# Attention with a top-32 mask and an MLP on one core: tile-major order with early MLP chunks, and two heads side by side on TensorE

## The chip, the cores and the metric

The kernel runs on one core of a Trainium2 chip. The metric is the time of one execution on the device, in microseconds (us). Three runs of the kernel before took 2404.17 to 2404.62 us, median 2404.35 us.

## The reference, cut to what matters

```python
# q, k, v: (8 batches, 8 heads, 576 tokens, 64), float32
scores = scale * np.matmul(q, k.transpose(0, 1, 3, 2))          # scale = 1/8
kth = np.partition(scores, -32, axis=-1)[..., -32:-32 + 1]      # the 32nd largest of each row
scores = np.where(scores >= kth, scores, -1000000000.0)
scores = scores - np.max(scores, axis=-1, keepdims=True)
attn = np.exp(scores)
attn = attn / (np.sum(attn, axis=-1, keepdims=True) + 1e-09)
x = np.matmul(attn, v)                                          # heads side by side: x is (4608, 512)
h = x @ w_in                                                    # w_in (512, 2048) and w_out (2048, 512), float64
g = np.where(h >= 1, h, np.where(h <= -1, 0.0, (h + 1) ** 2 / 4))
out = (g @ w_out).astype(np.float32)
```

## The kernel before

All products are float32. The eight batches are worked on as four pairs. Within a pair the loops run over four pairs of heads (`hp`), then nine tiles of 128 queries (`t`), then the two heads of the pair (`j`), so a step is one head of one tile, and there are 288 steps. Tile 4 holds the last 64 queries of the one batch and of the other. The parts of a step are spread over four turns of the main loop (from L285), so that several steps overlap:

- `scores` (L150): TensorE multiplies queries by keys in two halves of 288 keys with 64 rows of contraction, those of head `j` on partitions 64j to 64j + 63. ScalarE copies each half out of PSUM (L161). The PSUM tiles share four buffers, tag `mm`, with the first product of the MLP.
- `top_k` (L164): VectorE takes eight maxima (L171) and strikes them out (L175), four times over, for the 32 largest.
- `weights` (L179): ScalarE takes the exponential (L181); VectorE sets what lies under the 32nd value to zero and sums (L183), and takes the reciprocal of the sum (L187).
- `transpose_w` and `values` (L190, L200): TensorE transposes the weights in six pieces (L196), ScalarE copies them to `wT`, and TensorE multiplies them by the values with `wT` as the stationary operand (L205). ScalarE scales by the reciprocal (L210). After the second head of a pair `transpose_x` turns the 128 columns of `x` (L215).

The weights of the MLP arrive as 64-bit words. `weight_piece` (L68) makes float32 of 512 columns with six VectorE and five GpSimd instructions; there are 32 pieces. They are the side work of the first pair of batches. The MLP of a pair of batches (`mlp`, L219) works in three chunks of three tiles: 16 times four products into `ph` (L226), the activation on ScalarE, GpSimd and VectorE (L230 to L234), then 16 products per tile into `py` (L241). It is the side work of the next pair of batches' attention, and the last pair's MLP follows when all attention is done. `advance` (L271) deals out the side work by a rate.

The order in which each engine sees its instructions is set when the program is built: a scheduler puts instructions of the listing in order by its own estimate of times and by when buffers come free, and the engines then run their queues in that order.

Of the kernel before, what the change touches and what calls it, by code (L numbers as in the profile page):

```python
# [19 lines left out]
def kernel(  # L20
# [9 lines left out]
    """moe_w_in and moe_w_out are float64 arrays, seen as 64-bit integers; all else is float32."""  # L30
# [5 lines left out]
    assert D == 64 and S == 576 and DM == H * D == 512 and NTOK == B * S  # L36
    assert B % 2 == 0 and DFF % 512 == 0 and TOP_K % 8 == 0

    NP = B // 2              # pairs of batches: 1152 tokens, 9 tiles of 128
    NHP = H // 2             # pairs of heads: 128 columns of x  # L40
    NT = 2 * S // P          # query tiles of a pair of batches
    KC, KP = 6, 96           # keys of a head: chunk c, partition p is key KC * p + c
# [5 lines left out]
    NCH = NT // CT  # L48
    SCALE = float(D) ** -0.5

    const = ctx.enter_context(tc.tile_pool(name="const", bufs=1))
# [14 lines left out]
    WC = 512  # L66

    def weight_piece(pool, dst, src):  # L68
# [4 lines left out]
        # sign and top exponent bit, the low 7 exponent bits with 20 mantissa bits, 3 more  # L73
# [6 lines left out]
        # what the 29 bits left are worth: rest * 2^-52 * 2^exponent  # L80
# [4 lines left out]
        # 0 below float32's normal range, whose exponents these bits cannot say  # L85
# [23 lines left out]
    def load(bp, hp):  # L109
        b, h = 2 * bp, 2 * hp  # L110
        q_in = stage.tile([P, NT, 2, D], F32, name="q_in")
        k_in = stage.tile([KP, 2, KC, 2, D], F32, name="k_in")
        v_in = stage.tile([KP, 2, 2, KC, D], F32, name="v_in", bufs=2)
        for j in range(2):
# [5 lines left out]
            for i in range(2):  # L120
                nc.sync.dma_start(out=k_in[:, i, :, j, :], in_=k[b + i, h + j].rearrange("(p c) d -> p c d", p=KP))
# [163 lines left out]
    for m in range(n + 3):  # L285
# [20 lines left out]
        if m < n:  # L306
            top_k(state[m])
# [48 lines left out]
```

## Time and profile before

| | |
|---|---|
| median of three runs | 2404.35 us |
| profiled execution, first to last instruction | 2408.7 us |
| TensorE products (PE) busy | 2325.6 us, 97% |
| TensorE weight loads (PEld) busy | 1438.2 us, 60% |
| VectorE (DVE) busy | 1928.1 us, 80% |
| ScalarE (ACT) busy | 1005.0 us, 42% |
| GpSimd (POOL) busy | 430.8 us, 18% |
| chain of waits, by engine | PE 81%, DVE 12%, POOL 5% |

The span of 2408.7 us is the profiled execution's own time from its first instruction to its last, and it is 4.3 us above the median of the runs. Busy shares are averages over stretches with different limits. A busy PE is one with a product in flight, at whichever clock; the granted clock stands beside it in the slices and the stretches. A float32 product leaves two records, one per pass; a transpose leaves one.

### The profile page before, as it was taken

How to read it: one execution, taken by the hardware profiler on the slowest of the kernel's cores; microseconds unless marked ns; L12 is line 12 of the kernel's file. 1: busy time of each engine (PE TensorE's matmuls, PEld its weight loads, DVE VectorE, ACT ScalarE, POOL GpSimd, SP SyncE). 2: the span in 40 equal slices, each digit the busy share in tenths (PEclk: the TensorE clock that was granted, in tenths of full speed). 3: DMA queues.
4: the chain of work that ended last, by engine and by line, in shares of the span. 5: the costliest groups of instructions: out<-in, count | busy, mean ns of one | idle time of the engine just before them, and what ended most of it. 6: DMA issues, size and time to landing. Idle time of an engine off the chain costs nothing.

```text
span 2408.7 us, 29579 instructions
## 1 busy us (share of the span) xinstructions
PE 2325.6 (97%) x10016; PEld 1438.2 (60%) x10016; DVE 1928.1 (80%) x4416; ACT 1005.0 (42%) x2405; POOL 430.8 (18%) x647
## 2 busy tenths in 40 slices
PE   7888888999999999999999999999999999999999
PEld 4555555667665665655666656656666656565554
DVE  7889989988898898988898898889898988871100
ACT  3333333333544544544544544545545445432211
POOL 3554554200110100100100101101101102001210
PEclk6555555555999999999999999999999999999999
DMA  4111111000001000000000010000010000000000
GB/s 104 48 58 47 54 56 43 20 11 10 20 15 29 11 25 19 18 18 19 11 25 19 11 29 15 21 19 25 11 29 15 11 9 5 5 9 9 5 14 13
DMA packets 93399, 56.44 MB, mean 23 GB/s; under 512 B 78400, under 2 KB 84544, under 8 KB 93248
## 3 DMA queue, kind: packets, MB, share of 16 engines
q1 hardware_dynamic: 93248, 54.54, 8.0%
q8 instruction: 80, 1.31, 0.2%
q14 instruction: 71, 0.58, 0.1%
HBM read 45.09 MB, written 9.44 MB: 23 GB/s over the span
## 4 chain that ended last, share of the span: by engine, by line
PE 81%; DVE 12%; POOL 5%; issue 1%; ACT 0%; SPq 0%; DMA 0%; POOLq 0%; ACTq 0%; DVEq 0%
PE ph L226 21%; PE py L241 21%; PE po L205 15%; PE sp L158 14%; PE pw L196 8%; DVE tops L171 4%; DVE rest L175 3%; POOL low L93 2%; POOL low L92 2%; DVE w L183 2%; POOL keep L89 1%; PE px L215 1%; DVE top L76 1%; DVE top L78 1%; POOL low L91 1%
## 5 line engine op out<-in xcount | busy, mean ns | idle before, releaser
L171 DVE MAX8 tops<-rest 128x8 f32<-128x576 f32 x864 | 650.5, 753 | 8.0
L205 PEld LDWEIGHTS po<-v_in,wT 96*128 96x128 f32 (+1 forms) x3840 | 498.0, 212 | 134.4 <-ACT wT L197 116.9
L226 PE MATMUL ph<-xT,w_in 128*128 128x384 f32 x1536 | 551.9, 497 | 0.0
L241 PE MATMUL py<-w_out,g 128*128 128x512 f32 x1152 | 547.9, 604 | 2.1 <-ACT y L246 2.1
L205 PE MATMUL po<-v_in,wT 96*128 96x64 f32 (+1 forms) x3840 | 522.0, 299 | 2.9 <-ACT wT L197 2.8
L158 PE MATMUL sp<-kT,qT 64*128 64x288 f32 (+1 forms) x1280 | 500.3, 520 | 0.6 <-ACT g L232 0.4
L175 DVE MATCH_REPLACE8 rest<-tops,rest 128x576 f32<-128x576 f32 x576 | 427.7, 743 | 0.0
L226 PEld LDWEIGHTS ph<-xT,w_in 128*128 128x128 f32 x1536 | 274.6, 192 | 169.8 <-issue 31.4
L197 ACT COPY wT<-pw 96x384 f32<-96x384 f32 x576 | 252.8, 477 | 276.4 <-PE pw L196 274.7
L196 PEld LDWEIGHTS pw<-ident,w 128*96 128x96 f32 x1728 | 220.8, 143 | 218.1 <-issue 200.0
L196 PE MATMUL pw<-ident,w 128*96 128x128 f32 x1728 | 287.0, 311 | 64.0 <-DVE w L183 63.3
L234 DVE SCALAR_TENSOR_TENSOR g<-g,r 128x384 f32<-128x384 f32 x192 | 106.8, 556 | 279.3 <-POOL r L233 272.9
L241 PEld LDWEIGHTS py<-w_out,g 128*128 128x128 f32 x1152 | 200.0, 190 | 207.0 <-issue 197.7
L158 PEld LDWEIGHTS sp<-kT,qT 64*128 64x128 f32 (+1 forms) x1280 | 204.5, 204 | 167.4 <-issue 107.1
L171 DVE MAX8 tops<-s 128x8 f32<-128x576 f32 x288 | 215.0, 747 | 100.8 <-ACT s L161 100.6
L233 POOL TENSOR_TENSOR r<-r 128x384 f32<-128x384 f32 x192 | 163.8, 853 | 710.0 <-ACT r L230 706.0
L161 ACT COPY s<-sp 128x288 f32<-128x288 f32 x576 | 207.0, 407 | 190.4 <-DVE w L183 151.3
L173 POOL TENSOR_SCALAR nmax<-tops 128x1 f32<-128x1 f32 x288 | 61.7, 215 | 1084.8 <-DVE tops L171 1084.0
L181 ACT ACTIVATE w<-s,nmax 128x576 f32<-128x576 f32 x288 | 222.3, 772 | 80.2 <-POOL nmax L173 79.5
L210 ACT ACTIVATE x<-po,rz 128x64 f32<-128x64 f32 x288 | 90.1, 313 | 389.4 <-PE po L205 380.7
L183 DVE SCALAR_TENSOR_TENSOR w<-s,tops,w 128x576 f32<-128x576 f32 x288 | 245.3, 852 | 0.1
L175 DVE MATCH_REPLACE8 rest<-tops,s 128x576 f32<-128x576 f32 x288 | 213.7, 742 | 0.0
(37 smaller groups left out, 981.3 us busy)
## 6 DMA issues: line engine op xcount, KB each, us to landing
k_in<-in_k_dram SPq DMA_DIRECT2D x64, 144.0 KB, 3.0
v_in<-in_v_dram SPq DMA_DIRECT2D x32, 288.0 KB, 3.4
out_dram<-y SPq DMA_DIRECT2D x36, 256.0 KB, 2.3
q_in<-in_q_dram SPq DMA_DIRECT2D x64, 128.0 KB, 2.6
raw<-in_moe_w_in_dram SPq DMA_DIRECT2D x16, 512.0 KB, 3.7
raw<-in_moe_w_out_dram SPq DMA_DIRECT2D x16, 512.0 KB, 3.6
q_in<-in_q_dram SPq DMA_DIRECT2D x64, 16.0 KB, 2.1
```

Source lines behind the costliest of these rows:

```text
L158: nc.tensor.matmul(sp[r0:r1], qT[d0:d1, t, r0:r1], kT[d0:d1, i, 3 * hf:3 * hf + 3, :].rearrange("p c n -> p (c n)"), start=True, stop=True)
L161: nc.scalar.copy(s[:, hf * SH:(hf + 1) * SH], sp)
L171: nc.vector.max(out=tops[:, r:r + 8], in_=src)
L175: nc.vector.match_replace(out=rest, in_to_replace=tops[:, r:r + 8], in_values=src, imm_value=LOWEST)
L181: nc.scalar.activation(w, st["s"], AF.Exp, bias=st["nmax"], scale=SCALE)
L183: nc.vector.scalar_tensor_tensor(out=w, in0=st["s"], scalar=st["tops"][:, TOP_K - 1:TOP_K], in1=w, op0=ALU.is_ge, op1=ALU.mult, accum_out=z)
L196: nc.tensor.transpose(pt[:, c, :], w[:, (c0 + c) * KP:(c0 + c + 1) * KP], ident)
L197: nc.scalar.copy(wT[:, c0:c0 + 3, :], pt)
L205: nc.tensor.matmul(po[r0:r1], st["wT"][:, c, r0:r1], heads["v"][:, i, j, c, :], start=(c == 0), stop=(c == KC - 1))
L226: nc.tensor.matmul(ph, w_in[:, kk, f * P:(f + 1) * P], xT[:, kk, ch * CW:(ch + 1) * CW], start=(kk == 0), stop=(kk == NK - 1))
L233: nc.gpsimd.tensor_tensor(out=r, in0=r, in1=r, op=ALU.mult)
L241: nc.tensor.matmul(py, gs[f][:, i * P:(i + 1) * P], w_out[:, f, :], start=(f == 0), stop=(f == NF - 1))
```

## The change

A step is now two heads of one tile, and there are 144 steps. The order is tile-major: for one batch, each tile of 128 queries goes through its four pairs of heads before the next tile begins, so a tile's 512 columns of `x` are complete after four steps. The last 64 queries of two batches share a tile of `x`. An MLP chunk of up to three tiles starts when its tiles are done: the first after 12 steps, with the 32 weight pieces dealt out over those 12 steps. The remaining chunks follow one another as side work, the last with a single tile.

The two heads' scores are issued one after the other, on partitions 0 to 63 and 64 to 127, into two PSUM buffers of a tag of their own (`sc`). The mask is no longer a VectorE instruction: ScalarE applies a leaky rectifier to threshold minus score, with slope 2^-80 on the negative side, and then an exponential with scale -2^80, which gives zero for what lies under the threshold, and sums as it goes. The reciprocal of the sum goes into a diagonal matrix made by GpSimd, and the weights are transposed by an ordinary product with that matrix. In the product with the values the values are stationary, 64 columns per head, and the two heads write to partitions 0 to 63 and 64 to 127 of one PSUM tile; the result has the layout that the MLP wants, and `transpose_x` is gone. In the MLP the copy of `ph` by ScalarE is gone: VectorE reads `ph` from PSUM, and `ph` has two PSUM buffers of its own. The program holds one load of ScalarE's function table, as before.

```diff
-    xtp = ctx.enter_context(tc.tile_pool(name="xtp", bufs=2))
-    stage = ctx.enter_context(tc.tile_pool(name="stage", bufs=1))
-    qkt = ctx.enter_context(tc.tile_pool(name="qkt", bufs=2))
-    att = ctx.enter_context(tc.tile_pool(name="att", bufs=3))
+    xtp = ctx.enter_context(tc.tile_pool(name="xtp", bufs=3))
+    stage = ctx.enter_context(tc.tile_pool(name="stage", bufs=2))
+    att = ctx.enter_context(tc.tile_pool(name="att", bufs=2))
...
+    def keys_of(b):
+        kT = stage.tile([P, NHP, S], F32, name="kT")
...
+            for j in range(2):
+                nc.sync.dma_start(out=k_in[:, :, j, :], in_=whole(k, b)[:, 2 * hp + j])
+            pt = ps.tile([P, NT, P], F32, name="pk", tag="tr", bufs=2)
+            for c in range(NT):
+                nc.tensor.transpose(pt[:, c, :], k_in[:, c].rearrange("p j d -> p (j d)"), ident)
+            nc.scalar.copy(kT[:, hp, 0:SM], pt.rearrange("p c n -> p (c n)"))
...
+            yield dict(kT=kT, v=v_in, v_tl=v_tl)
...
+    def scores(st):
+        t, hp, kT, qT = st["t"], st["hp"], st["keys"]["kT"], st["qT"]
+        st["s"] = s = att.tile([P, 2, S], F32, name="s", bufs=4)
+        for hf in range(2):
+            keys = slice(hf * SH, (hf + 1) * SH)
+            sp = [ps.tile([P, SH], F32, name="sp", tag="sc", bufs=2) for _ in range(2)]
             for i in range(2):
+                for j in ([i] if t < NT else [0, 1]):
+                    d = slice(j * D, (j + 1) * D)
+                    g = hp if t < NT else hp + i
+                    o = sp[i] if t < NT else sp[i][j * TL:(j + 1) * TL]
+                    nc.tensor.matmul(o, qT[d, g, :], kT[d, g, keys], start=True, stop=True)
+            for i in range(2):
+                nc.scalar.activation(s[:, i, keys], sp[i], AF.Copy, scale=SCALE)
...
     def weights(st):
-        w = att.tile([P, S], F32, name="w")
-        nc.scalar.activation(w, st["s"], AF.Exp, bias=st["nmax"], scale=SCALE)
-        z = att.tile([P, 1], F32, name="z")
-        nc.vector.scalar_tensor_tensor(out=w, in0=st["s"], scalar=st["tops"][:, TOP_K - 1:TOP_K], in1=w,
-                                       op0=ALU.is_ge, op1=ALU.mult, accum_out=z)
-        rz = att.tile([P, 1], F32, name="rz")
+        s, tops = st["s"], st["tops"]
+        nb = att.tile([P, 2], F32, name="nb")
+        nc.gpsimd.tensor_tensor(out=nb, in0=tops[:, :, TOP_K - 1], in1=tops[:, :, 0], op=ALU.subtract)
+        z = att.tile([P, 2], F32, name="z")
+        for i in range(2):
+            nc.scalar.activation(s[:, i, :], s[:, i, :], AF.Prelu, bias=tops[:, i, TOP_K - 1:TOP_K], scale=-1.0,
+                                 alpha=1.0 / FAR)
+            nc.scalar.activation(s[:, i, :], s[:, i, :], AF.Exp, bias=nb[:, i:i + 1], scale=-FAR,
+                                 accum_out=z[:, i:i + 1])
+        rz = att.tile([P, 2], F32, name="rz")
         nc.vector.tensor_scalar(z, z, 1e-9, None, ALU.add)
         nc.vector.reciprocal(rz, z)
-        st["w"], st["rz"] = w, rz
+        st["diag"] = diag = att.tile([P, 2, P], F32, name="diag")
+        for i in range(2):
+            nc.gpsimd.tensor_scalar(diag[:, i, :], ident, rz[:, i:i + 1], 1.0, ALU.mult, ALU.mult)
...
     def transpose_w(st):
...
+        t, w, diag = st["t"], st["s"], st["diag"]
+        st["wT"] = wT = att.tile([P, 2, NT, P], F32, name="wT")
+        st["wTt"] = wTt = att.tile([P, P], F32, name="wTt")
+        for i in range(2):
+            pt = ps.tile([P, NT, P], F32, name="pw", tag="tr", bufs=2)
+            for c in range(NT):
+                nc.tensor.matmul(pt[:, c, :], w[:, i, c * P:(c + 1) * P], diag[:, i, :], start=True, stop=True)
+            nc.scalar.copy(wT[:, i], pt)
+        pt = ps.tile([P, P], F32, name="pwt", tag="po")
+        for i in range(2):
+            if t < NT:
+                nc.tensor.matmul(pt[i * TL:(i + 1) * TL], w[:, i, SM:S], diag[:, i, :], start=True, stop=True)
...
+        nc.scalar.copy(wTt, pt)
...
     def values(st):
-        t, j, heads = st["t"], st["j"], st["heads"]
-        po = ps.tile([P, D], F32, name="po", tag="po")
-        for r0, r1, i in rows_of(t):
-            for c in range(KC):
-                nc.tensor.matmul(po[r0:r1], st["wT"][:, c, r0:r1], heads["v"][:, i, j, c, :],
-                                 start=(c == 0), stop=(c == KC - 1))
-        if j == 0:
-            heads["x"] = att.tile([P, P], F32, name="x", bufs=2)
-        st["x"] = x = heads["x"]
-        nc.scalar.activation(x[:, j * D:(j + 1) * D], po, AF.Copy, scale=st["rz"])
...
+        t, hp, v_in, v_tl = st["t"], st["hp"], st["keys"]["v"], st["keys"]["v_tl"]
+        wT, wTt = st["wT"], st["wTt"]
+        po = ps.tile([P, P], F32, name="po", tag="po")
+        if t < NT:
+            for c in range(NT + 1):
+                for j in range(2):
+                    h = 2 * hp + j
+                    nc.tensor.matmul(po[j * D:(j + 1) * D], v_in[:, h, c, :] if c < NT else v_tl[:, h, :],
+                                     wT[:, j, c, :] if c < NT else wTt, start=(c == 0), stop=(c == NT))
...
+    def mlp(xT, tiles, pool):
+        cw = len(tiles) * P
+        gs = []
+        for f in range(NF):
+            ph = ps.tile([P, CW], F32, name="ph", tag="ph", bufs=2)[:, 0:cw]
+            for kk in range(NK):
+                nc.tensor.matmul(ph, w_in[:, kk, f * P:(f + 1) * P], xT[:, kk, 0:cw],
+                                 start=(kk == 0), stop=(kk == NK - 1))
+            r = pool.tile([P, CW], F32, name="r", bufs=2)[:, 0:cw]
+            nc.scalar.activation(r, ph, AF.Relu, bias=half, scale=0.5)
+            g = pool.tile([P, CW], F32, name="g", bufs=NF)
+            nc.gpsimd.tensor_tensor(out=r, in0=r, in1=r, op=ALU.mult)
+            nc.vector.scalar_tensor_tensor(out=g[:, 0:cw], in0=ph, scalar=1.0, in1=r, op0=ALU.max, op1=ALU.min)
+            gs.append(g)
+            yield
...
+    rounds, chunks = [], []
+    for b in range(0, B, 2):
+        a, c, tl = [(b, t) for t in range(NT)], [(b + 1, t) for t in range(NT)], (b, NT)
+        if b + 2 < B:
+            rounds += a + [tl] + c + [(b + 1, NT)]
+            chunks += [a[0:3], a[3:4] + c[0:2], c[2:4] + [tl]]
+        else:
+            rounds += a + [tl, (b + 1, NT)] + c
+            chunks += [a[0:3], a[3:4] + [tl] + c[0:1], c[1:3], c[3:4]]
...
+    begin(0)
+    next_keys = 1
+    for m in range(n + 2):
         if m < n:
             top_k(state[m])
+        if m + 1 < n:
+            begin(m + 1)
         if 1 <= m <= n:
             weights(state[m - 1])
-        if 2 <= m <= n + 1:
+        if 2 <= m:
             transpose_w(state[m - 2])
         advance(rate / 2)
-        if 2 <= m <= n + 1:
...
+        if 2 <= m:
             values(state[m - 2])
-        advance(rate / 2)
-        if 3 <= m:
-            transpose_x(state[m - 3])
-            if (m - 2) % per_bp == 0:
-                done = (m - 2) // per_bp
+            state[m - 2] = None
+            for ch in [c for c in range(len(chunks)) if ready[c] == m - 2]:
                 for _ in side:
                     pass
                 if mlp_pool is None:
                     cvt.__exit__(None, None, None)
                     mlp_pool = ctx.enter_context(tc.tile_pool(name="mlp", bufs=1))
-                side, due, rate = mlp(done - 1, xTs[done - 1], mlp_pool), 0.0, n_units / (per_bp - 2)
-            state[m - 3] = None
+                side, due = mlp(xTs[ch], chunks[ch], mlp_pool), 0.0
+                rate = units[ch] / (ready[ch + 1] - ready[ch]) if ch + 1 < len(chunks) else 0.0```

Two places show how the instructions move. The first is TensorE in the middle of the program. Before, the weights of one head (`pw`), the two halves of scores (`sp`) and one head's values (`po`) alternate with MLP products (`ph`), and only the first `pw` and the first `po` of a group wait:

```order
L196 MATMUL pw<-ident,w 96x128 [waits DVE_49,PE_49]
L196 MATMUL pw<-ident,w 96x128 x2
L196 MATMUL pw<-ident,w 96x128 [waits Activation_49]
L196 MATMUL pw<-ident,w 96x128 x2
L158 MATMUL sp<-kT,qT 128x288
L205 MATMUL po<-v_in,wT 128x64 [waits Activation_49]
L205 MATMUL po<-v_in,wT 128x64 x2
L205 MATMUL po<-v_in,wT 128x64 [waits Activation_49]
L205 MATMUL po<-v_in,wT 128x64 x2
L158 MATMUL sp<-kT,qT 128x288 x3
L226 MATMUL ph<-xT,w_in 128x384 [waits Activation_49]
L226 MATMUL ph<-xT,w_in 128x384 x2
```

Now a whole step of two heads stands in twelve rows (`pwt` is the last 64 keys of the weights):

```order
L181 MATMUL sp<-kT,qT 128x288 x2
L181 MATMUL sp<-kT,qT 128x288 [waits Activation_49] x2
L226 MATMUL pw<-diag,s 128x128 [waits Pool_49]
L226 MATMUL pw<-diag,s 128x128 x3
L226 MATMUL pw<-diag,s 128x128 [waits Pool_49]
L226 MATMUL pw<-diag,s 128x128 x3
L231 MATMUL pwt<-diag,s 64x128 [waits PE_49]
L231 MATMUL pwt<-diag,s 64x128
L277 MATMUL ph<-xT,w_in 128x384 x4
L247 MATMUL po<-wT,v_in 64x128 [waits Activation_49]
L247 MATMUL po<-wT,v_in 64x128 x7
L247 MATMUL po<-wTt,v_tail_79 64x128 x2
```

The second pair of score products now waits for ScalarE to empty the two buffers of the first pair. Of the 132 steps from the first MLP product on, 55 have the second pair directly behind the first, as here, and most of the others have one to four `pw` products in between.

The second place is GpSimd while the weights are converted. Before, one piece (L91 to L94) lies between the small products for the maxima (`nmax`) of one or two steps:

```order
L91 TENSOR_SCALAR low<-rest 128x512
L92 TENSOR_TENSOR low<-low,unit 128x512
L89 TENSOR_SCALAR keep<-keep 128x512
L93 TENSOR_TENSOR low<-low,top 128x512
L94 TENSOR_TENSOR w_in<-low,keep 128x512
L173 TENSOR_SCALAR nmax<-tops 128x1 x2
L91 TENSOR_SCALAR low<-rest 128x512
L92 TENSOR_TENSOR low<-low,unit 128x512
L89 TENSOR_SCALAR keep<-keep 128x512
L93 TENSOR_TENSOR low<-low,top 128x512
L94 TENSOR_TENSOR w_in<-low,keep 128x512
L173 TENSOR_SCALAR nmax<-tops 128x1
```

Now two or three pieces follow one another before the small difference (`nb`) and the two diagonals of a step:

```order
L96 TENSOR_SCALAR low<-rest 128x512
L94 TENSOR_SCALAR keep<-keep 128x512
L97 TENSOR_TENSOR low<-low,unit 128x512
L98 TENSOR_TENSOR low<-low,top 128x512
L99 TENSOR_TENSOR w_in<-low,keep 128x512
L96 TENSOR_SCALAR low<-rest 128x512
L94 TENSOR_SCALAR keep<-keep 128x512
L97 TENSOR_TENSOR low<-low,unit 128x512
L98 TENSOR_TENSOR low<-low,top 128x512
L99 TENSOR_TENSOR w_in<-low,keep 128x512
L204 TENSOR_TENSOR nb<-tops 128x2
L216 TENSOR_SCALAR diag<-ident,rz 128x128 x2
```

All 32 pieces stand on GpSimd before the first MLP square (L283) of the program.

## Rows read from the trace of the kernel before

**Rows 1.** Page, busy tenths and granted clock in 40 slices of 60.2 us

```profile
PE   7888888999999999999999999999999999999999
DVE  7889989988898898988898898889898988871100
PEclk6555555555999999999999999999999999999999
```

**Rows 2.** Stretches: length, busy us of PE, PEld, DVE, ACT, POOL; clock, DMA

```profile
0.00:440.00 440.00, 364.51 (x1301) 247.38 (x1302) 388.42 (x895) 151.63 (x356) 218.04 (x219) 0.53 0.20 58
440.00:600.00 160.00, 159.97 (x561) 109.80 (x562) 137.21 (x317) 61.81 (x156) 4.81 (x23) 0.50 0.05 12
606.00:2157.00 1551.00, 1548.85 (x7473) 950.54 (x7472) 1371.55 (x3150) 739.25 (x1786) 168.24 (x357) 1.00 0.06 17
2157.00:2409.00 252.00, 246.28 (x668) 126.27 (x666) 26.81 (x48) 51.36 (x106) 39.74 (x48) 1.00 0.03 10
```

**Rows 3.** Timeline of PE, first MLP product: start us, us, instructions

```profile
598.88 1.49 PE L226 MATMUL ph<-xT,w_in 128*128 128x384 f32 x2
```

**Rows 4.** Waits in order of time, start of the program and of conversion

```profile
8.03 2.36 PE pq L133 x9
16.40 0.77 DVE tops L171
31.59 0.33 DVE top L75
```

**Rows 5.** Groups by line, GpSimd and VectorE, while weights are converted and after

```profile
L173 POOL TENSOR_SCALAR nmax<-tops 128x1 f32<-128x1 f32 x288 | 61.7, 215 | 1084.8 <-DVE tops L171 1084.0
L91 POOL TENSOR_SCALAR low<-rest 128x512 f32<-128x512 uint32 x32 | 20.5, 642 | 126.6 <-DVE rest L84 126.5
L75 DVE TENSOR_SCALAR top<-raw 128x512 uint32<-128x512 uint32 x32 | 14.0, 438 | 32.9 <-POOL low L93 32.9
L76 DVE SCALAR_TENSOR_TENSOR top<-raw,top 128x512 uint32<-128x512 uint32 x32 | 22.4, 699 | 0.0
L234 DVE SCALAR_TENSOR_TENSOR g<-g,r 128x384 f32<-128x384 f32 x192 | 106.8, 556 | 279.3 <-POOL r L233 272.9 <-ACT g L232 3.4 <-ACT s L161 1.9
```

**Rows 6.** Timeline of PE in one step, MLP running beside it

```profile
1302.30 0.82 PE L196 MATMUL pw<-ident,w 128*96 128x128 f32 x6
1302.95 0.81 PE L226 MATMUL ph<-xT,w_in 128*128 128x384 f32 x2
1303.60 1.45 PE L205 MATMUL po<-v_in,wT 96*128 96x64 f32 x12
1304.89 0.42 PE L140 MATMUL pk<-ident,k_in 96*128 96x96 f32 x3
1305.23 0.75 PE L158 MATMUL sp<-kT,qT 64*128 64x288 f32 x2
1305.91 0.33 PE L215 MATMUL px<-ident,x 128*128 128x128 f32 x1
```

**Rows 7.** Timeline of PE where score products of two heads or batches meet

```profile
1028.50 0.70 PE L158 MATMUL sp<-kT,qT 64*64 64x288 f32 x4
1029.14 1.12 PE L241 MATMUL py<-w_out,g 128*128 128x512 f32 x2
...
1644.39 1.25 PE L158 MATMUL sp<-kT,qT 64*128 64x288 f32 x8
1645.63 0.91 PE L226 MATMUL ph<-xT,w_in 128*128 128x384 f32 x2
...
2121.67 1.23 PE L158 MATMUL sp<-kT,qT 64*128 64x288 f32 x4
2122.84 1.12 PE L241 MATMUL py<-w_out,g 128*128 128x512 f32 x2
```

**Rows 8.** Groups by line, ScalarE: copy of half the scores, and the exponential

```profile
L161 ACT COPY s<-sp 128x288 f32<-128x288 f32 x576 | 207.0, 407 | 190.4 <-DVE w L183 151.3 <-PE sp L158 27.6 <-PE ph L226 8.3
L181 ACT ACTIVATE w<-s,nmax 128x576 f32<-128x576 f32 x288 | 222.3, 772 | 80.2 <-POOL nmax L173 79.5
```

**Rows 9.** Waits in order of time, VectorE's searches and strikings

```profile
325.13 0.73 DVE rest L175 x2
325.93 1.32 DVE tops L171 x2
```

More of the change, by code (lines that the diff above doesn't have):

```diff
@@ L145, in rows_of, with whole @@
[L145 to L162 removed]
+    def whole(x, b):
+        return x[b, :, 0:SM, :].rearrange("h (p c) d -> p h c d", c=NT)
@@ L257 @@
-    steps = [(bp, hp, t, j) for bp in range(NP) for hp in range(NHP) for t in range(NT) for j in range(2)]
-    per_hp, per_bp = 2 * NT, 2 * NT * NHP
-    n_pieces = NK * DFF // WC + NF * DM // WC
-    n_units = NCH * (NF + CT * (NF // 4))
-    loads = [load(0, 0)]
-    heads, xTs = [], []
-    state = []
-    side, due, rate = None, 0.0, 0.0
+        t, w, diag = st["t"], st["s"], st["diag"]
+        st["wT"] = wT = att.tile([P, 2, NT, P], F32, name="wT")
+        st["wTt"] = wTt = att.tile([P, P], F32, name="wTt")
@@ new lines, in rows_of @@
+    def rows_of(b, t):
+        r0 = b * S
+        if t < NT:
+            return [(0, P, out[r0:r0 + SM, :].rearrange("(p c) n -> p c n", c=NT)[:, t, :])]
+        return [(i * TL, (i + 1) * TL, out[r0 + i * S + SM:r0 + (i + 1) * S, :]) for i in range(2)]
+    def mlp(xT, tiles, pool):
[13 more added lines that the diff above has]
+            yield
+        for i, (b, t) in enumerate(tiles):
+            py = ps.tile([P, DM], F32, name="py", tag="py")
+            for f in range(NF):
+                nc.tensor.matmul(py, gs[f][:, i * P:(i + 1) * P], w_out[:, f, :],
+                                 start=(f == 0), stop=(f == NF - 1))
+                if f % 4 == 3 and f < NF - 1:
+                    yield
+            y = pool.tile([P, DM], F32, name="y", bufs=2)
+            nc.scalar.copy(y, py)
+            for p0, p1, rows in rows_of(b, t):
+                nc.sync.dma_start(out=rows, in_=y[p0:p1])
+            yield
@@ new lines @@
+    rounds, chunks = [], []
[4 more added lines that the diff above has]
+            chunks += [a[0:3], a[3:4] + c[0:2], c[2:4] + [tl]]
+        else:
+            rounds += a + [tl, (b + 1, NT)] + c
+            chunks += [a[0:3], a[3:4] + [tl] + c[0:1], c[1:3], c[3:4]]
+    steps = []
+    for b, t in rounds:
+        tile_of = (b, t) if t < NT else (b - b % 2, t)
+        ch = next(n for n, tiles in enumerate(chunks) if tile_of in tiles)
+        col = chunks[ch].index(tile_of) * P + (TL if t == NT and b % 2 else 0)
+        for hp in (range(NHP) if t < NT else range(0, NHP, 2)):
+            steps.append((b, t, hp, ch, col))
@@ L266 @@
+    n = len(steps)
+    ready = [max(m for m in range(n) if steps[m][3] == ch) for ch in range(len(chunks))]
+    units = [NF + len(tiles) * (NF // 4) for tiles in chunks]
+    n_pieces = NK * DFF // WC + NF * DM // WC
     cvt = tc.tile_pool(name="cvt", bufs=1)
@@ L273, in advance @@
         due += amount
[L274 removed]
+        while due >= 1.0:
             due -= 1.0
             next(side, None)
[L278 to L305 removed]
@@ new lines, with fetch, begin @@
+    keys, xTs = {}, {}
+    q_ins, qTs = {}, {}
+    def fetch(i):
+        if i < len(rounds) and rounds[i] not in q_ins:
+            q_ins[rounds[i]] = load_queries(*rounds[i])
+    fetch(0)
+    for got in keys_of(0):
+        keys[0] = got
+    fetch(1)
+    prep = None
+    state = []
+    def begin(m):
+        b, t, hp, ch, col = steps[m]
+        if (b, t) not in qTs:
+            qTs[b, t] = queries_of(q_ins[b, t], t)
+            fetch(rounds.index((b, t)) + 2)
+        if ch not in xTs:
+            xTs[ch] = xtp.tile([P, NK, CW], F32, name="xT")
+        state.append(dict(t=t, hp=hp, keys=keys[b], qT=qTs[b, t], xT=(xTs[ch], col)))
+        scores(state[m])
```

216 lines of the change are left out of this document (81 added, 135 removed).

## The prediction

> **What bounds the kernel now.** I read the slices of the page first, then stretches, then TensorE's timeline inside one step. The slices [rows 1] show two regimes: about a quarter of the span at a granted clock of 5 to 6 tenths, then TensorE at nine tenths or more and full clock to the end, with VectorE almost as busy until the last three slices. The stretches [rows 2] give the limits. From 0 to 440 us the weights are converted beside attention: VectorE is busy 388 of 440 us and GpSimd half. From 440 to 600 us TensorE has a product in flight the whole time at a clock of 0.50 (the 1.2 GHz level), with only attention in its queue. The first MLP product starts at 598.88 us [rows 3], and the clock is 1.00 (2.4 GHz) in the stretch from 606 on. From there to 2157 us TensorE is busy 1548.85 of 1551 us: it is the bound. The last 252 us are the MLP of nine tiles alone. So before has 600 us in which no MLP product runs and a quarter of the attention is done, and some 1803 us bounded by TensorE.
>
> **What one step costs on TensorE at full clock.** The start-to-start distances in one step [rows 6]: six weight transposes take 1302.30 to 1302.95, 0.65 us, 0.108 us each; the MLP's two records of 384 columns 0.65 us; twelve records of values 1303.60 to 1304.89, 1.29 us; one half of the scores 1305.23 to 1305.91, 0.68 us. Four records of 288 columns of the same kind take 1.17 us (2121.67 to 2122.84), so one product takes 1.17 − 0.68 = 0.49 us and there is 0.19 us of leaving the 64-row form [rows 7].
>
> **The pairs.** Does "side by side" hold? Before has both kinds by accident [rows 7]. Eight records (four products: both halves of two heads, on different partitions) take 1644.39 to 1645.63, 1.24 us, against 1.17 us for the four records of one head. Four records of 64 output rows (tile 4, two halves of PSUM partitions) take 0.64 us, no longer than the two records at 1305.23 [rows 6]. So pairs in different row halves and in different column halves run together, in float32, at full clock.
>
> **The change, part by part.**
>
> 1. Scores: two pairs per step. Unsplit 1.24 us, split by other work twice 0.68; I take 1.35 with the way in.
> 2. Weight transposes: eight ordinary products of 128 columns, two passes each instead of one: 16 × 0.108 = 1.73 us, and for the last 64 keys one pair of products, 2 × 0.108 = 0.22. Before paid 2 × 0.65 = 1.30 per two heads, so this part is dearer.
> 3. Values: ten products of 128 columns, two passes, in pairs: 10 × 0.108 = 1.08 us against 2 × 1.29 = 2.58. For going into and out of the column halves twice a step no row stands alone; between nothing and the 0.19 us each way of the scores, twice in and out 0 to 0.76; I take 0.4, the middle.
> 4. `transpose_x` goes: 0.11 us per two heads.
>
> Sum 1.35 + 1.73 + 0.22 + 1.08 + 0.4 = 4.8 us. The same bookkeeping falls short in before: of the 1551 us, 27 tiles of MLP at 246.28/9 = 27.4 us take 739, leaving 812 for 216 head-steps, 3.76 us each; by rows [rows 6] a head is 2 × 0.68 + 0.65 + 1.29 + 0.06 (half a `transpose_x`) + 0.11 (its share of some 250 query and key transposes) = 3.47. Of the missing 0.29 per head, 0.58 per two, I carry over 0.45 per step, since a step has no `transpose_x` to go in and out of: 5.25 us.
>
> 5. Early MLP. The first 12 steps carry all 32 conversions. GpSimd in the first 440 us is busy 218.04 us over 219 instructions; 160 are the conversions' five each, some 55 are the small products at 0.215 us [rows 2, 5], so a piece costs (218 − 12)/32 = 6.45 us and all 207 us. Added on GpSimd per step: a small difference (0.215) and two diagonals of 128 columns, each between that 0.215 and the 0.642 us of a 512-column scalar operation [rows 5]; with 0.3 each 0.8 us, 11 us in 13 steps. VectorE's `top` waits for GpSimd, 32.9 us in before over 32 pieces [rows 5]; closer packing can only keep that or raise it, and GpSimd waits for VectorE in turn; I add 24. Conversions begin when the first loads are through: before starts transposing at 8.03 and converting at 31.59 [rows 4]; now the first raw piece stands behind a dozen loads, one of 1 MB, and I take 20. First MLP product at 20 + 207 + 11 + 24 = 262 us, with 238 as the floor (no waits). The ceiling is VectorE's: 13 steps at 10 us (below), 32 × 6 operations at no more than 0.699 and twice 32.9 us of waiting: 20 + 130 + 134 + 66 = 350. TensorE is not the bound there: 12 steps at half clock are 12 × 10.5 = 126 us.
>
> 6. After that, TensorE has 36 tiles of MLP, 36 × 27.4 = 985 us, 132 steps × 5.25 = 693, and some 290 query and key transposes × 0.108 = 31: 1709 us.
>
> 7. New wait: the scores have two PSUM buffers instead of four shared ones. The second pair waits until ScalarE has copied the first, two copies of 0.407 us [rows 8] plus the way out, about 1.0 us. Behind it in TensorE's queue stand the transposes and all that follows. In 55 of the 132 steps nothing lies between the pairs: 55 us; in the others one to four `pw` products (0.22 to 0.86 us) cover part: 77 × 0.35 = 27. Together 82 us; nothing, if other engines' slack hid it, is the low end, and 132 × (1.0 + 2 × 0.77) the high one, if one exponential or rectifier [rows 8] is ahead of each copy.
>
> 8. VectorE: two searches 1.32 us, strike-out with its value load 0.73 [rows 9], so a step of two heads is 8 × 0.66 + 6 × 0.73 = 9.7, with the two small operations 10 us; the mask's 0.8 per head goes. With 192 × 0.556 for the MLP [rows 5] that is 262 + 132 × 10 + 107 = 1690 us: not the bound, and it covers the waits of 5 by itself. ScalarE gains the rectifier, 288 × 0.772 = 222 us [rows 8], and loses copies; about 1100 us, off the path but for point 7.
>
> 9. The end: one tile of MLP whose products wait in turn for ScalarE, GpSimd and VectorE, and the last store; before leaves 252 − 246.28 = 6 us idle in its last stretch [rows 2]; I take 10.
>
> Sum: 262 + 1709 + 82 + 10 = 2063 us of span. The runs' median lies 4.3 us under the profiled span, so 2059; I say 2058.
>
> The Trainium skill, TensorEngine Tiling (Array Packing), section Tiling Modes, says that changing the tiling mode drains TensorE. Rows 7 agree for scores (0.19 us). By that rule every change of form would cost it, the columns too: 0.76 in place of 0.4 per step, 132 × 0.36 = 48 us more, about 2106.
>
> **Rivals.**
>
> A. ScalarE's emptying of PSUM becomes the pace. For: two buffers, and a copy stands in one queue with rectifiers and exponentials that wait for VectorE. Against: by point 8 ScalarE is busy about half the time. Price: 132 × 2 × 0.772 = 204 us more, about 2260. The Trainium skill, same page, section Performance Considerations, warns that tiling speeds up TensorE but not the emptying of PSUM, which may become the limit. No row of before shows that, since there the products don't run in pairs by design.
>
> B. The pairs don't run together in the new form, full 128-row contraction above all, which before never has in column halves. Values alone: 132 × 1.08 = 143 us, 2200; scores (2 × 0.49) and the last keys too: 132 × 2.28 = 301, 2360.
>
> C. Better than forecast: the wait of 7 hidden, nothing unaccounted (4.8 us a step), first MLP product at the floor: 238 + 985 + 634 + 31 + 10 = 1898.
>
> D. Slower: the clock. If MLP products spread among attention do not hold 2.4 GHz, TensorE's 1709 us lengthen by one us for each us of work done at 1.2 GHz. From 2404 − 2058 = 346 us of such work, a fifth, the kernel is slower than before; at a quarter, 2058 + 427 = 2485. For: from 440 to 600 us a full queue of attention alone stayed at 0.50 [rows 2]. Against: the clock was up within about 7 us of the first MLP product and the next 1551 us show 1.00 [rows 2, 3], with MLP 739 of 1551 us; now it is 985 of about 1790, a larger share.
>
> **How the numbers follow.** Forecast (TensorE-bound, pairs together, 1960 to 2170): 0.60. A: 0.15. B: 0.07. C and what lies between it and the forecast: 0.12. D: 0.06. The range 1900 to 2260 leaves out half of A, most of B, D and little of C, 0.2 in all. A change under 0.2% cannot be told from none here. Only D makes it slower: 0.05 slower, 0.02 the same, 0.93 faster.
>
> **What would show it right or wrong.** The first MLP product near 262 us; the clock at 1.00 soon after and to the end; TensorE busy throughout with short gaps before `sp` put down to ScalarE; a score pair taking no longer than one product; VectorE idle about a fifth of the time. Wrong: VectorE at nine tenths with TensorE waiting for it, values' records one after the other, a clock that falls back, or a first MLP product past 350 us.

## The result and the profile after

The changed kernel takes 2151.36 us (median of four runs, 2151.0 to 2151.82), 0.8944 of the time before, 95% interval 0.8932 to 0.8957: 253 us less. The forecast was 2058, range 1900 to 2260: right in sign and inside the range, 93 us too low.

The slices, against [rows 1] (a slice is now 53.75 us):

```profile
PE   4333459999999999999999999999999999999999
DVE  5888799978768779878768779878678779767530
PEclk9756779999999999999999999999999999999999
```

TensorE is full from the seventh slice on and the granted clock stays at its upper level; VectorE has room. The same in stretches, columns as in [rows 2]:

```profile
0.00:304.00 304.00, 116.25 (x652) 84.96 (x652) 239.73 (x484) 87.29 (x199) 242.50 (x205) 0.72 0.29 79
304.00:440.00 136.00, 131.98 (x807) 79.01 (x804) 131.49 (x295) 80.91 (x188) 26.63 (x55) 1.00 0.08 21
606.00:1560.00 954.00, 936.39 (x5166) 554.11 (x5165) 763.38 (x1664) 496.87 (x1158) 144.47 (x310) 1.00 0.08 20
2117.00:2150.00 33.00, 28.79 (x166) 20.40 (x162) 4.67 (x16) 6.74 (x18) 6.41 (x16) 0.97 0.05 17
```

For 304 us GpSimd and VectorE are busy four fifths of the time each and TensorE 38%; then TensorE is the bound. Its timeline where the first stage ends answers to [rows 3]:

```profile
264.28 1.56 PE L277 MATMUL ph<-xT,w_in 128*128 128x384 f32 x4
...
299.97 3.79 PE L226 MATMUL pw<-diag,s 128*128 128x128 f32 x16 [10.18 <-POOL diag L216]
...
306.82 0.91 PE L277 MATMUL ph<-xT,w_in 128*128 128x384 f32 x2
```

The first MLP product starts at 264.28 us, where 262 was forecast. But four records are no full queue: weight transposes that wait for `diag` stand ahead of the next ones, and TensorE is full from 306 on. The groups of GpSimd's first 310 us say why (busy us, mean ns of one | idle us before, and whom it waited for):

```profile
L94 POOL TENSOR_SCALAR keep<-keep 128x512 f32<-128x512 f32 x32 | 60.5, 1892 | 7.3 <-DVE keep L92 7.3
L216 POOL TENSOR_SCALAR diag<-ident,rz 128x128 f32<-128x128 f32 x24 | 27.5, 1154 | 2.2 <-DVE rz L213 1.9
L96 POOL TENSOR_SCALAR low<-rest 128x512 f32<-128x512 uint32 x32 | 26.5, 827 | 17.8 <-DVE rest L89 16.2
L204 POOL TENSOR_TENSOR nb<-tops 128x2 f32<-128x2 f32 x13 | 4.0, 310 | 28.6 <-ACT s L207 14.6 <-DVE tops L192 8.4 <-DVE z L212 5.6
```

A diagonal takes 1.15 us here; later, without conversion beside it, the same instruction takes a third:

```profile
L216 POOL TENSOR_SCALAR diag<-ident,rz 128x128 f32<-128x128 f32 x208 | 75.3, 375 | 225.9 <-PE pwt L231 102.0 <-PE pwt L234 49.2 <-PE pw L226 23.2
```

One step of two heads on TensorE beside the MLP, against [rows 6, 7]:

```profile
1001.11 0.76 PE L181 MATMUL sp<-kT,qT 64*128 64x288 f32 x4
1001.80 0.94 PE L226 MATMUL pw<-diag,s 128*128 128x128 f32 x6
1002.82 1.05 PE L181 MATMUL sp<-kT,qT 64*128 64x288 f32 x4
1003.80 1.38 PE L226 MATMUL pw<-diag,s 128*128 128x128 f32 x10
1005.11 0.44 PE L231 MATMUL pwt<-diag,s 128*64 128x128 f32 x4
1005.48 5.43 PE L277 MATMUL ph<-xT,w_in 128*128 128x384 f32 x16
1010.84 1.09 PE L247 MATMUL po<-wT,v_in 128*64 128x128 f32 x16
1011.76 0.39 PE L247 MATMUL po<-wTt,v_tail 128*64 128x128 f32 x4
1012.08 2.85 PE L277 MATMUL ph<-xT,w_in 128*128 128x384 f32 x8
1014.86 0.76 PE L181 MATMUL sp<-kT,qT 64*128 64x288 f32 x4
```

I read each row from its start to the start of the next. Four score records of two heads take 0.69 us, where four of one head took 1.17; 16 records of values 0.92, or 0.058 each where one alone takes 0.108: the pairs run together. The second score pair takes 0.98, a wait inside. And `ph` x16 takes 5.36, `ph` x8 2.78: the eight records more cost 0.322 each, so 0.2 us goes with each visit of the MLP, for the change from and to a form in halves (products with 64 rows or 64 columns).

Adding up such distances by tile, from 306 us to the last record of a product, gives for the whole program:

| us | forecast | after |
|---|---|---|
| TensorE full from | 262 | 306 |
| MLP (`ph` 524.2, `py` 515.8) | 985 | 1040.0 |
| query and key transposes | 31 | 30.3 |
| steps, score wait included (`sp` 257.5, `pw` 290.7, `po` 167.9, `pwt` 52.9) | 693 + 82 | 769.0 |
| end | 10 | 4.4 |

### The profile page after: what moved, and what is told of

Read it like the earlier page. It is cut to its first block, busy times and chain, and to the rows that moved or that the text cites. A ratio compares the mean times of both kernels' runs of the same rounds, so it can differ in the third digit from the quotient of the medians.

```text
span 2150.0 us, 29200 instructions
## 1 busy us (share of the span) xinstructions
PE 1923.7 (89%) x10560; PEld 1158.1 (54%) x10560; DVE 1649.7 (77%) x3568; ACT 1008.3 (47%) x2341; POOL 527.1 (25%) x809
## 2 busy tenths in 40 slices
PE   4333459999999999999999999999999999999999
DVE  5888799978768779878768779878678779767530
## 4 chain that ended last, share of the span: by engine, by line
PE 67%; DVE 19%; ACT 5%; POOL 5%; issue 3%; DMA 0%; SPq 0%; POOLq 0%; ACTq 0%; DVEq 0%
PE py L290 20%; PE ph L277 19%; PE pw L226 10%; PE sp L181 9%; DVE tops L192 8%; DVE rest L195 7%; PE po L247 5%; ACT s L183 2%; PE pwt L231 2%; POOL keep L94 1%; POOL low L98 1%; POOL low L97 1%; ACT s L207 1%; ACT s L209 1%; ACT r L281 1%
## 5 line engine op out<-in xcount | busy, mean ns | idle before, releaser
L192 DVE MAX8 tops<-rest 128x8 f32<-128x576 f32 x864 | 614.5, 748 | 0.1
L277 PE MATMUL ph<-xT,w_in 128*128 128x384 f32 (+2 forms) x1664 | 543.1, 472 | 2.3 <-DVE g L284 2.3
L226 PE MATMUL pw<-diag,s 128*128 128x128 f32 x2304 | 345.3, 298 | 163.5 <-POOL diag L216 163.5
L226 PEld LDWEIGHTS pw<-diag,s 128*128 128x128 f32 x2304 | 296.9, 202 | 256.6 <-POOL diag L216 173.4
L277 PEld LDWEIGHTS ph<-xT,w_in 128*128 128x128 f32 x1664 | 293.4, 190 | 183.9 <-issue 21.6
L207 ACT ACTIVATE s<-s,tops 128x576 f32<-128x576 f32 x288 | 217.1, 774 | 339.5 <-DVE tops L192 329.2
L283 POOL TENSOR_TENSOR r<-r 128x384 f32<-128x384 f32 (+2 forms) x208 | 161.8, 778 | 638.1 <-ACT r L281 638.1
L192 DVE MAX8 tops<-s 128x8 f32<-128x576 f32 x288 | 208.0, 750 | 143.7 <-ACT s L183 143.5
L181 PE MATMUL sp<-kT,qT 64*128 64x288 f32 x1024 | 241.6, 464 | 39.3 <-ACT s L183 34.0
L183 ACT ACTIVATE s<-sp 128x288 f32<-128x288 f32 x576 | 210.7, 408 | 94.8 <-PE sp L181 89.5
L209 ACT ACTIVATE s<-s,nb 128x576 f32<-128x576 f32 x288 | 223.0, 775 | 1.5 <-POOL nb L204 0.4
L227 ACT COPY wT<-pw 128x512 f32<-128x512 f32 x288 | 167.2, 585 | 91.9 <-PE pw L226 90.8
L181 PEld LDWEIGHTS sp<-kT,qT 64*128 64x128 f32 x1024 | 115.7, 188 | 150.1 <-ACT s L183 79.8
L216 POOL TENSOR_SCALAR diag<-ident,rz 128x128 f32<-128x128 f32 x288 | 123.0, 440 | 288.2 <-PE pwt L231 134.0
L204 POOL TENSOR_TENSOR nb<-tops 128x2 f32<-128x2 f32 x144 | 29.9, 208 | 655.2 <-DVE tops L192 243.8
L247 PEld LDWEIGHTS po<-wT,v_in 128*64 128x64 f32 x2048 | 111.8, 138 | 71.5 <-issue 58.7
```

Source lines behind the costliest of these rows:

```text
L181: nc.tensor.matmul(o, qT[d, g, :], kT[d, g, keys], start=True, stop=True)
L183: nc.scalar.activation(s[:, i, keys], sp[i], AF.Copy, scale=SCALE)
L192: nc.vector.max(out=tops[:, i, r:r + 8], in_=src[:, i, :])
L207: nc.scalar.activation(s[:, i, :], s[:, i, :], AF.Prelu, bias=tops[:, i, TOP_K - 1:TOP_K], scale=-1.0, alpha=1.0 / FAR)
L209: nc.scalar.activation(s[:, i, :], s[:, i, :], AF.Exp, bias=nb[:, i:i + 1], scale=-FAR, accum_out=z[:, i:i + 1])
L226: nc.tensor.matmul(pt[:, c, :], w[:, i, c * P:(c + 1) * P], diag[:, i, :], start=True, stop=True)
```

## Experiments

Unless another kernel is named, each is the changed kernel with the edit shown, and its difference is to 2151.36 us.

**Scores from one half of the rows (e1).**

```diff
-                    d = slice(j * D, (j + 1) * D)
+                    d = slice(0, D) if t < NT else slice(j * D, (j + 1) * D)
```

> Both heads' scores are computed from the rows of the first head (partitions 0 to 63), so the second head's part of the output is that of wrong scores; every engine has the same instructions in the same order. If a score pair in the changed kernel really runs side by side, it now takes two products in turn: 0.49 us more a pair (1.17 - 0.68 in the rows of the kernel before), two pairs in each of 132 steps, 129 us; ScalarE then empties the first buffer while the second product runs, which can hide up to 65 us of the waits for it: +64 to +129, I say +100, about 2250. A row of four score records takes 1.17 us in place of 0.68. Rival (pairs never ran together, or TensorE is not the pace): no change, 2151.

Measured 2191.02, +39.7. Four records now take 1.17 us, and TensorE's wait for ScalarE ahead of `sp`, 34.0 us in the changed kernel, is gone. The timeline:

```profile
1018.09 1.23 PE L181 MATMUL sp<-kT,qT 64*128 64x288 f32 x4
1019.26 0.94 PE L226 MATMUL pw<-diag,s 128*128 128x128 f32 x6
```

and of that wait (us, times, longest) there is left

```profile
PE sp L181 <- ACT s L183: 0.3, 1, 0.3
```

The pairs are side by side in the changed kernel. The size fell below the stated bounds, and these were too high: the edit leaves the steps of the last 64 queries alone, 16 of the 132, so 116 × 0.98 = 114 us of products come in and not 129. Of these, 114 − 40 = 74 us lie where TensorE waited before.

**Values head after head (e2).**

```diff
-            for c in range(NT + 1):
-                for j in range(2):
+            for j in range(2):
+                for c in range(NT + 1):
```

> The values' products of one head now all stand ahead of those of the other head; same products, same order of all else. If only products that stand next to each other in the queue run side by side, ten records of 0.108 us are added per step: 132 x 1.08 = +143, about 2294, and a row of ten records takes 1.1 us in place of 0.55. If TensorE looks further along its queue than the next product, part of it stays hidden. Rival (pairs never ran together in this form): no change, 2151.

Measured 2222.63, +71.3. One step's values:

```profile
1011.59 1.15 PE L247 MATMUL po<-wT,v_in 128*64 128x128 f32 x10
1012.51 0.27 PE L247 MATMUL po<-wTt,v_tail 128*64 128x128 f32 x1
...
1012.68 0.71 PE L247 MATMUL po<-wT,v_in 128*64 128x128 f32 x5
1013.23 0.38 PE L247 MATMUL po<-wTt,v_tail 128*64 128x128 f32 x2
1013.54 2.85 PE L277 MATMUL ph<-xT,w_in 128*128 128x384 f32 x8
```

That is 1.95 us in place of 1.24. This edit too leaves 16 steps alone: 0.71 × 116 = 82 us of stream (the distances of `po` rise from 167.9 to 250.9), not the 143 expected, and 71 of them reach the total. The pairs are real in this form too (rival B falls). Where one head's records meet the other's, some still overlap.

**Diagonals on ScalarE (e5).**

```diff
-            nc.gpsimd.tensor_scalar(diag[:, i, :], ident, rz[:, i:i + 1], 1.0, ALU.mult, ALU.mult)
+            nc.scalar.activation(diag[:, i, :], ident, AF.Copy, scale=rz[:, i:i + 1])
```

> The two diagonal matrices of a step are made by ScalarE and no longer by GpSimd. In the trace of the changed kernel GpSimd spends 27.5 us on 24 diagonals (1154 ns each) while it converts weights, and the first MLP product starts at 287 us. If the diagonals are what delays the start, the first MLP product comes at 255 to 262 us and the total falls as much, 25 to 32 us, to about 2122. Rival 1: conversion is paced by VectorE and GpSimd waiting for each other, and the start stays within 8 us of 287. Rival 2: ScalarE now waits for the reciprocal with the copies of scores queued behind it, which gives back after the start what was won: total 2145 or more, though the start is early.

Measured 2149.26, −2.1. The 287 us of the expectation are the MLP's second visit (287.34); its first is at 264.28. Here they stand at 278.07 and 255.58, and TensorE is full from 296.5 in place of 306: the start comes 9 to 10 us earlier, not 25 to 32, so most of the delay is not the diagonals'. GpSimd lost 27.5 us of diagonals, but its `low`, 827 ns before, now takes

```profile
L96 POOL TENSOR_SCALAR low<-rest 128x512 f32<-128x512 uint32 x32 | 40.7, 1273 | 23.5 <-DVE rest L89 21.8
```

which gives 14 us back, and its waits ahead of `low` grew by 6. After the start TensorE loses 6 us again, mostly at `sp`, so the total is that of the second rival; that ScalarE's queue is the reason was not tried.

**Four shared PSUM buffers (e6).**

```diff
-name="sp", tag="sc", bufs=2
+name="sp", tag="mm", bufs=4
...
-name="ph", tag="ph", bufs=2
+name="ph", tag="mm", bufs=4
```

> Scores and the first MLP product share four PSUM buffers, as before the change, in place of two each. In the trace of the changed kernel some 95 us after the start of the MLP are score products that wait for ScalarE to empty one of two buffers. If two buffers are the cause, most of it goes: 60 to 95 us less, about 2075. Rival: scores then wait behind MLP tiles that share the buffers, or the pace is set elsewhere: 2140 to 2160.

Measured 2096.61, −54.8, a little under the range. The distances of `sp` fall from 257.5 to 218.8 us, those of `pw` by 18. The score wait is real, and two buffers are its cause. But the order of TensorE's queue changes with the buffers: score products stand in 139 rows, where they stood in 219, so some 80 × 0.2 = 16 of the 55 us are changes of form and not waits (an estimate from the 0.2 us above).

**Weights scaled first (e9).**

```diff
+                nc.gpsimd.tensor_scalar(s[:, i, :], s[:, i, :], rz[:, i:i + 1], 1.0, ALU.mult, ALU.mult)
...
-                nc.tensor.matmul(pt[:, c, :], w[:, i, c * P:(c + 1) * P], diag[:, i, :], start=True, stop=True)
+                nc.tensor.transpose(pt[:, c, :], w[:, i, c * P:(c + 1) * P], ident)
```

> The weights themselves are multiplied by the reciprocal of their sum (by ScalarE in the first 13 steps, by GpSimd after), and the eight 128-column transposes of a step are transposes of one record each, as in the kernel before, in place of products with a diagonal of two. If TensorE's stream is the pace, 8 records of 0.11 us go in each of 132 steps: 118 us less, about 2030. Rival 1: the transposes now wait for GpSimd, which scales 576 columns in place of 128: the gain is under 60 us and TensorE shows gaps ahead of pw put down to GpSimd. Rival 2: TensorE is not the pace: 2140 to 2160.

Measured 2040.11, −111.3; `pw` falls from 290.7 to 155.7 us, and waits ahead of `sp` take back a part (257.5 to 276.9). TensorE is full some 10 us earlier, as in e5, since GpSimd makes no diagonals. So the transposes as products with a diagonal cost the change 111 us, about 100 of them in TensorE's stream.

**Last keys of both heads together (e10, on e9).**

```diff
...
+        if t < NT:
+            nc.tensor.transpose(pt, w.rearrange("p i n -> p (i n)")[:, SM:SM + P], ident)
```

> As the kernel that scales first, and the second head's last 64 keys are stored ahead of its other 512, so that the last keys of both heads are 128 neighbouring columns: their transpose is one record with 128 output columns in place of four records in two column halves. Compared with the kernel that scales first, in some 117 steps from the first MLP product on: if going in and out of column halves costs 0.2 and 0.16 us as read from the distances between rows, (0.36 + 0.22 - 0.11) x 117 = 55 us less. If the form changes cost nothing, only 0.11 x 117 = 13 us less.

Measured 1992.67, 47.4 less than e9. `pwt` falls from 56.3 to 19.3 us, and no other tile by more than 6. Without a price on the change of form 13 were expected, with it 55. The trace has the price in the MLP's rows too: eight `py` records behind `pwt`, now in full form, take 3.53 us, and eight behind `po`, in halves, 3.63.

```profile
715.47 0.27 PE L240 MATMUL pwt<-ident,s 128*128 128x128 f32 x1
715.58 3.60 PE L300 MATMUL py<-w_out,g 128*128 128x512 f32 x8
719.11 1.09 PE L257 MATMUL po<-wT,v_in 128*64 128x128 f32 x16
720.03 0.39 PE L257 MATMUL po<-wTt,v_tail 128*64 128x128 f32 x4
720.35 3.70 PE L300 MATMUL py<-w_out,g 128*128 128x512 f32 x8
723.98 0.76 PE L188 MATMUL sp<-kT,qT 64*128 64x288 f32 x4
```

Record by record (medians, start to start), a `py` record takes 0.429 us within a row, and the first behind `pwt` 0.533 in e9 and 0.432 here; for `ph` it is 0.322, 0.427 and 0.325.

**Late MLP (e4).**

```diff
-n_pieces / (ready[0] + 1)
+n_pieces / (ready[1] + 1)
...
-            for ch in [c for c in range(len(chunks)) if ready[c] == m - 2]:
+            for ch in [c - 1 for c in range(1, len(chunks)) if ready[c] == m - 2]:
...
```

> The changed kernel with one thing other: the weight pieces are dealt out over the first 24 steps in place of 12, and each MLP chunk starts when the next chunk is ready. The TensorE theory: a step without MLP beside it goes at VectorE's pace (9.8 us and its share of conversion), one with MLP at TensorE's. The first MLP chunk then starts at about 400 us, 120 steps follow beside MLP: 400 + 1027 + 120 x 5.8 + 10 = 2133, and with the 50 us by which this sum falls short of the changed kernel, 2185 (+35). Rival: each us by which the MLP starts later is a us of the total, 2250 or more.

Measured 2154.0, +2.6. TensorE is full from 403.52 us, 97 later, and 14 steps more lie ahead of that:

```profile
120.00:180.00 60.00, 35.13 (x234) 25.67 (x230) 57.03 (x126) 26.50 (x63) 43.33 (x39) 0.77 0.21 57
```

VectorE is busy 57.03 of 60 us there (48.98 in the changed kernel), so a step more costs 97/14 = 6.9 us, hardly more than beside the MLP: 769.0/132 = 5.8 us, and its share of the MLP's changes of form. Both numbers expected were too high, and the rival falls: between these two starts, how early the first chunk begins is worth next to nothing by itself.

**Mask on VectorE (e3).**

```diff
...
+            nc.scalar.activation(w, s[:, i, :], AF.Exp, bias=nb[:, i:i + 1])
+            nc.vector.scalar_tensor_tensor(out=s[:, i, :], in0=s[:, i, :], scalar=tops[:, i, TOP_K - 1:TOP_K],
+                                           in1=w, op0=ALU.is_ge, op1=ALU.mult, accum_out=z[:, i:i + 1])
```

> The changed kernel with the mask back on VectorE: ScalarE takes one exponential, VectorE compares with the 32nd value, multiplies and sums (0.8 us a head in the kernel before); y has one buffer in place of two. VectorE gains 1.6 us a step, 230 us in all, 1650 + 230 = 1880 of some 2150. If TensorE is the pace after the start, only the 13 steps of conversion lengthen: up to 21 us, 2150 to 2172. Rival: the mask's move is a part of the gain by itself, and the steps with MLP lengthen by the 1.6 us or half of it: 2255 or more.

Measured 2182.23, +30.9, above the forecast 21 and far from the rival: TensorE is full 24 us later (from 330), and after that its distances add up to 6 us more.

**All three (e11).** e10 with the four shared buffers of e6.

> The kernel with the tails together (scaled first, one-record transposes, last keys of both heads as neighbours), and scores and first MLP product share four PSUM buffers. In the changed kernel the shared buffers took away 55 us. If the score wait is the same wait here, 40 to 60 us less than the kernel with the tails together: 1935 to 1950. Rival: VectorE, busy 270 of 300 us from 600 to 900 us there, is now the pace in part, and less than 20 us go: 1972 or more.

Measured 1959.05, 33.6 less than e10 and between the two theories. The chain that ended last shows the next bound, by engine:

```profile
DVE 54%; PE 25%; ACT 9%; POOL 8%; issue 3%; DMA 0%; SPq 0%; POOLq 0%; ACTq 0%; DVEq 0%
```

In the changed kernel it was PE 67%, DVE 19%.

**Values by the scores (e12, on e11).** `values(state[m - 3])` stands behind `begin(m + 1)`, ahead of `weights`, and the loop has one turn more.

> The kernel with all three edits, and the values' products of a step follow directly behind the scores of a later one (one step further on), with the whole share of the MLP between transposes and scores. Per step TensorE then changes form three times (MLP to scores, scores to values, values to transposes) in place of four. If each change costs about 0.2 us, 132 x 0.2 = 26 us less than the kernel with all three. If what counts is only how long TensorE streams, no change within 8 us. Rival on the other side: the MLP no longer lies between a step's parts, and TensorE waits for ScalarE's copies ahead of pw or values: 20 us more.

Measured 1955.79, ratio to before 0.8128 (0.8115 to 0.8140) against 0.8141 (0.8130 to 0.8152) for e11: not told apart. The changes of form did go: from 306 us on, MLP rows border on a row in halves 173 times, where they did 403 times in e11, which at 0.1 us each is some 23 us. A new wait took the place: `pwt` waits for the copy of `po`, whose buffer it shares.

```profile
PE pwt L240 <- ACT xT L270: 27.2, 35, 2.3
```

**Comparison on VectorE in the conversion (e13, on e11).** Four of the conversion's tiles get two buffers besides.

```diff
-        nc.gpsimd.tensor_scalar(keep, keep, 1.125 * 2.0 ** -15, None, ALU.is_ge)
...
-        nc.gpsimd.tensor_tensor(out=dst, in0=low, in1=keep, op=ALU.mult)
+        nc.vector.scalar_tensor_tensor(out=dst, in0=keep, scalar=1.125 * 2.0 ** -15, in1=low, op0=ALU.is_ge, op1=ALU.mult)
```

> The kernel with all three edits, and in the conversion of weights the comparison and the last multiplication are one VectorE instruction in place of two on GpSimd (1.89 and 1.41 us a piece there, 105 us in all; about 0.7 us a piece, 22 us, added on VectorE); four of the conversion's tiles have two buffers. If GpSimd sets the pace of the first 306 us, VectorE takes over: its 244 us of work there, 22 more and 18 before the first piece give some 285 us, about 20 us less of total. Rival: VectorE was the pace already, and the total rises by up to 22 us.

Measured 1993.51, 34.5 more than e11. Both theories miss: TensorE is full from 328 us, in e11 from 296. The moved instruction waits for GpSimd, and VectorE's searches stand behind it in the queue (us, times, longest):

```profile
DVE w_in L98 <- POOL low L97: 27.4, 12, 3.2
DVE w_out L98 <- POOL low L97: 25.6, 12, 3.2
```

**Two buffers for the conversion (e14, on e12).** All five working tiles get `bufs=2`; `pwt` takes `tag="tr"`.

> The kernel with the values by the scores and two edits more. All of the conversion's working tiles have two buffers, so VectorE does not wait for GpSimd to let go of the one (39 us in the first 300 us there). pwt takes its PSUM buffer from the pair of the other transposes and not the one of the values, whose copy it waited for (29 us). Read by stage: if the single buffers delay the start of the MLP, TensorE is full from 270 to 285 us on in place of some 306. If GpSimd's own 240 us of work and its waits for ScalarE set that time, it stays within 8 us of 306. After the start, 15 to 29 us go if TensorE is still the pace; under 10 if VectorE is. Together, from 1956: 1895 to 1920 if both theories hold, 1945 or more if neither does.

Measured 1955.98: no gain, so neither theory holds. In the first 310 us VectorE waits less for GpSimd (39.0 us in e12, 15.4 here), but its six instructions of the 32 pieces take 143.9 us where they took 120.4, and GpSimd's five 237.7 where they took 227.5:

```profile
60.00:120.00 60.00, 17.83 (x99) 13.32 (x101) 60.00 (x112) 22.05 (x49) 52.45 (x38) 0.58 0.22 68
```

VectorE is busy throughout this stretch (the third figure of busy time). And GpSimd's group:

```profile
L96 POOL TENSOR_SCALAR low<-rest 128x512 f32<-128x512 uint32 x32 | 58.2, 1818 | 19.3 <-DVE rest L89 19.2
```

The MLP's stream begins at 296.68 us, in e12 at 295.81; the 306 of the expectation is the changed kernel's. After that `pwt` waits for the copy of `wT` in place of that of `po`.

## Why the prediction was right in kind and 93 us low

- **The bound.** TensorE's stream sets the time once it is full: records taken away (e9) or added (e2) show in the total, the mask's 1.6 us a step on VectorE (e3) hardly. Rival D did not come: the clock is 1.00 in every stretch from 304 to 2117 us.
- **Pairs (parts 1, 3).** They run together, in both forms; e1 and e2 take this away, and the time rises by 40 and 71 us.
- **Step and score wait (parts 1 to 4 and 7).** 775 us were forecast, 769 measured, and that they agree so closely is in part luck. For 132 steps `pw` was forecast at 228 us and took 291, `pwt` 29 and 53, `po` 195 and 168; `sp` with its wait 260 and 258. The 59 us that were carried over from before, without a row to show what they are, made it up. The score wait was forecast at 82 us; e6 takes away 55, changes of form included, and e1 fills 74. Rival A falls, since buffers take most of the wait away (e6) and ScalarE is busy 47%.
- **Early MLP (part 5): the first mis-sized term, +44 us.** That the first MLP product came at 264, where 262 was forecast, is luck. The sum of part 5 adds up to the time when GpSimd has converted the last piece, and that is 306.5 us; the first product needs less and came before it, and the sum of the whole needs the time from which TensorE is full, 306. Term by term: 18 us to the first piece (20 forecast); 213.3 for the five groups of 32 pieces (207, [rows 2, 5]); 31.5 for the small differences and the diagonals (11), since a diagonal took 1.15 us and not 0.3; and 43 of waiting (24), of which 28.6 at `nb` for ScalarE and VectorE, while VectorE waits 32.1 for GpSimd at `top` and 13.4 at `rest`. No edit to the conversion or the diagonals brought the start forward by more than 10 us (e5, e13, e14). e4 shows besides that the start is no term by itself: a later start with more steps ahead of it costs the same.
- **MLP (part 6): the second, +55 us.** 27.4 us a tile came from MLP that runs alone. Among attention, the first MLP record behind a row in halves takes 0.10 us more and the last ahead of one 0.09 (0.523 for 0.429, 0.416 for 0.322); ahead of the key transposes, in full form, it takes what it takes within a row. From 306 us on there are 278 such beginnings and 228 such ends, together some 50 us. The prediction priced changes of form in the steps alone (0.4 for values, 0.45 unaccounted). e10 shows the price by an edit: 47 us for one row in column halves a step, 13 of them stream. The Trainium skill, TensorEngine Tiling (Array Packing), section Tiling Modes, says that a change of mode drains TensorE; this trace agrees, columns included. The prediction's 2106 by that rule had the price in the values' rows, where it was missed in the MLP's; that 2106 and the 44 us of the late start make 2150 is in part luck.
- **The rest.** The steps and the end took 6 us less each than forecast. The prediction took 5 us off to get from the span to the median; after the change the median lies 1.4 us above the span.
- **VectorE and ScalarE (part 8).** VectorE is busy 1649.7 us (1690 forecast), ScalarE 1008.3 (1100), its rectifier 774 ns where [rows 8] gave 772: off the path, as said, until e9, e10 and e6 together take 192 us from TensorE.

What stays open is which of GpSimd's and VectorE's instructions lengthen each other, and with it what would shorten the first 306 us; no run isolates a pair. The Trainium skill, SBUF — State Buffer, section SBUF: two separate sides, says that the two engines share a pair of ports and that an instruction holds it whole while the other engine's blocks, for VectorE instructions in a two-port mode or with two SBUF inputs. The durations in e14 agree with that: VectorE's waits for GpSimd fell by 23.6 us, and its conversion instructions grew by 23.5.

## What to carry to other kernels

Forecast the time from which the bounding engine has a full queue, not the first instruction of the stage that it bounds. Price each change of TensorE's form, also in the rows of the work that it interrupts: here about 0.1 us for the record before it and 0.1 for the one behind. A faster stream shows its next wait at once: give tiled products as many PSUM buffers as cover their copies, and don't pay a second pass on TensorE for a scaling that an idle engine can do (e11 takes 1959 us, 0.8141 of before, 0.8130 to 0.8152).

## What the runs showed of the hardware that was not expected

- One GpSimd instruction (`low`, 512 columns) takes 0.642 us [rows 5], 0.827 in the changed kernel, 1.273 in e5 and 1.818 in e14, each time beside VectorE at other work; the diagonal takes 0.375 or 1.154 (that VectorE lengthens them is argued, not shown). In e14 VectorE lengthens too, its third `top` instruction from 676 ns (e12) to

```profile
L83 DVE SCALAR_TENSOR_TENSOR top<-raw,top 128x512 uint32<-128x512 uint32 x32 | 32.4, 1011 | 0.0
```

- Products of two column halves overlap not only with their next neighbour, if TensorE's queue has them as the edit does: in e2 records of both heads alternate where the two runs of ten meet.
- The price of a change of form stands on the records at the border and does not grow with their length: 0.10 and 0.09 us at records of 384 columns as of 512 (the changed kernel), nothing behind a transpose in full form (e10).
